# A planner's lengths split into occupation and latency, and VectorE's share of an attention set by a table

## The chip, the cores and the metric

The kernel runs on one core of a Trainium2 chip. The metric is device microseconds of one execution; the median of three runs of the kernel before is 1753.39 us (1752.82 to 1754.59).

## The reference

Four blocks are applied to a residual stream `x` of 2048 tokens by 512 features in bf16: attention, gated mixer, attention, gated mixer, with the same weights both times. Cut to what matters:

```python
def attention(x):            # 32 query heads of 16, one shared key and value head
    q, k, v = heads(x @ wq), x @ wk, x @ wv
    p = softmax(q @ k.T * 16 ** -0.5)          # 32 heads x 2048 x 2048
    return merge(p @ v) @ wo

def mixer(x):                # F = 1792, Fh = 896
    z = gelu(x @ w_in)
    z1, z2 = z[:, :896], layernorm(z[:, 896:])
    g = w_sp @ z2 + b_sp[:, None]              # w_sp is 2048 x 2048
    return (z1 * g) @ w_out

for _ in range(2):
    x = x + attention(layernorm(x))
    x = x + mixer(layernorm(x))
```

The bulk is the exponential of 2 x 32 x 2048 x 2048 scores.

## The kernel before

**Groups and units.** In each layer the attention's queries are cut into 32 groups (`GROUPS`), and each group is worked off in 16 units, one for every 128 keys. A unit is four blocks of 128 keys x 512 query columns, and TensorE computes the four blocks' scores side by side in four row strips of its array (L800). Groups 0 to 3 of a layer (`attn_first`, L975) are interleaved with the projection of keys and values; their partial sums go to an accumulator in SBUF. Groups 4 to 31 follow in `attn_rest` (L991). A group's products with V are summed in one PSUM bank (`PVB`), so that groups follow each other there, and VectorE copies the finished sum out (L923, L926, L932 or L935), after which a short chain normalises and turns it (L902, L908, L917, L945, L948).

**Two ways to take the exponential.** A unit on ScalarE goes through `push_unit` and `push_slot`: blocks are put alternately into a slot of three PSUM banks and one of two, ScalarE takes `Exp` of 1536 or 1024 columns into `P_ring` (L824, a ring of 20 blocks), and TensorE multiplies by V (L841), one step of four matmuls to a unit. A unit on VectorE goes through `push_unit_dve` (L859): the scores go through one of the two side banks, VectorE adds a bias and clamps to an integer of 16 bits (L872, four instructions), makes four further versions with other offsets (L881, four instructions of 128x2048), and TensorE multiplies all five by differently weighted copies of V (L887), five steps of four matmuls. The bits of the integers are read as bf16, and the five together approximate the exponential. The five tiles come from a ring of six (five for the last groups) in `big`.

Which units of a group go to VectorE is given by `UNITS` (the places of 0 to 4 units among the 16) and `ON_DVE` (how many in each group): none in groups 0 to 3, three in 4 to 23, two in 24 to 31. `FIRST_DVE` adds one unit to each of the groups 0 to 3. That is 80 units in a layer and 160 in all.

**Other work under the attention.** The mixer's first products run under the attention as soon as their tokens are done (`b_front`, L1028; evacuated at L1051 and L1077). The product with `w_sp` runs in two stages (`mix_stage`, L1137): stage 0 may start after group 11, stage 1 after group 23. Each stage makes 28 tiles of six steps of four matmuls on TensorE (L613), which VectorE adds up (L1176) and a DMA on SP's queue writes to a scratch tensor (L1178). They have the lowest priority. What remains, and `gelu_rest` and `mix_late`, forms the handover between the layers and the tail after the last one.

**Who orders the work.** The kernel is not written in the order in which it runs. Each operation is recorded with an engine, a length `dur`, a latency `lat`, a priority and the keys that it reads and writes. `schedule` (L174) then plays the whole program through with these lengths before anything is built: an engine that is free takes the ready operation of the best priority (`pick`, L256), a PSUM task takes its banks when they are free in that playing (`banks_for`), and an operation counts as finished for others at its start plus `dur` plus `lat` plus `SEM_LAT` (0.06). The order so found is emitted as each engine's fixed program, with semaphore waits for the real dependencies. The lengths therefore decide the order alone; on the chip an engine waits at the head of its program for whatever is late. Where TensorE has nothing ready and has worked less than 55% of the last 3.4 us of the playing, `filler` (L287) puts in a matmul without effect (L631, L636, and L639 in four strips).

The lengths that matter here: VectorE's operations have their whole length as `dur` and no latency (`dve`, L590). An `Exp` of n blocks has `0.065 + n * 0.4267` and no latency; a PSUM bank comes free in the playing when the task's last operation counts as finished (L386).

Of the kernel before, what the change touches and what calls it, by code (L numbers as in the profile page):

```python
# [10 lines left out]
ALU = mybir.AluOpType  # L11
# [28 lines left out]
SEM_LAT = 0.06  # L40
BESIDE = 0.03

HOLDS = 2.5


# [30 lines left out]
class _Op:  # L76
    __slots__ = ("eng", "fn", "dur", "lat", "prio", "seq", "deps", "succ", "nleft", "chan", "chan_val",
                 "inc", "pos", "val", "clock", "t0", "task", "mode", "rows", "work", "opens", "nstart", "due", "chain")

    def __init__(self, eng, fn, dur, lat, prio, seq, chan, task, mode):  # L80
        self.task = task
        self.mode = mode
        self.rows = frozenset()
        self.work = dur
        self.opens = None
        self.eng = eng
        self.fn = fn
        self.dur = dur
        self.lat = lat
        self.prio = prio  # L90
        self.seq = seq
        self.deps = {}
        self.succ = []
        self.nleft = 0
        self.chan = chan
        self.chan_val = 0
        self.inc = False
        self.pos = -1
        self.val = 0
        self.clock = None  # L100
        self.t0 = -1.0
        self.chain = False
        self.nstart = 0
        self.due = 0.0


class _Graph:
# [66 lines left out]
    def schedule(self):  # L174
# [154 lines left out]
        while True:  # L329
            moved = True  # L330
            while moved:
                moved = False
                for e in ENGS:
                    if free[e]:
# [24 lines left out]
                        push(now + us, 0, e)  # L359
                        push(now + us + o.lat + SEM_LAT, 1, o)  # L360
                        at = now + us + o.lat + SEM_LAT
                        for s, k in o.succ:
# [10 lines left out]
            while ev and ev[0][0] <= now + 1e-9:  # L373
# [3 lines left out]
                elif what == 1:  # L377
                    for s, k in x.succ:
                        if k == 1:
                            met(s, x)  # L380
                    t = x.task
                    if t is not None:
                        t.left -= 1
                        if t.left == 0:
                            for b in t.banks:
                                bank_free[b] = True  # L386
        assert done == len(self.ops), (done, len(self.ops))
# [74 lines left out]
def bass_interleave_layers__grouped_kv_mqa__mixer_gmlp__prompt_kernel(  # L462
# [127 lines left out]
    def dve(fn, us, r, w, prio=5):  # L590
        return op("dve", fn, us, r=r, w=w, prio=prio)

# [210 lines left out]
    def push_slot(n):  # L803
# [19 lines left out]
        def act_e(e):  # L823
            return e.activation(P_ring[:, s0:s0 + n, :], bank32(b0, n).rearrange("p (k q) -> p k q", k=n), ACTF.Exp,  # L824
                                scale=E_SCALE)
        main["last"] = op("act", act_e, 0.065 + n * 0.4267, r=[tk], w=[("P", s0 + k) for k in range(n)], prio=3)
        for k, (u, j) in enumerate(blocks):
# [31 lines left out]
    def push_unit_dve(u):  # L859
# [6 lines left out]
        for j in range(4):  # L866
# [6 lines left out]
                ph16[:, tiles[0], j * QC:(j + 1) * QC], bank32(tk.bank), PH_BIAS, 0.0, op0=ALU.add, op1=ALU.max),  # L873
                0.66, [tk], BIG(tiles[0]) if j == 0 else [("phj", tiles[0], j)], P_R)
            if j == 0:
# [4 lines left out]
        for a in range(1, NPH):  # L880
            dve(lambda e, a=a: e.tensor_scalar(ph16[:, tiles[a], :], ph16[:, tiles[0], :], float(PH_A[a]), None,  # L881
                                               op0=ALU.add), 0.63, base, BIG(tiles[a]), 4)
        for a in range(NPH):
# [107 lines left out]
    def attn_rest():  # L991
        phr["base"] = 0
        for gi in range(NFIRST, len(GROUPS)):
            on_dve = UNITS[ON_DVE[gi]]
            phr["ring"] = NRING if gi < SHORT_RING else NPH
# [285 lines left out]

    UNITS = {0: (), 1: (4,), 2: (3, 8), 3: (2, 6, 10), 4: (2, 5, 8, 11)}

# [4 lines left out]
    NFIRST = 2 * CHUNKS[0][1]  # L1288
    FIRST_DVE = ({12: (2,)}, {12: (2,)})
    KEYS = ((0, 2), (2, 2), (4, 4), (8, 4), (12, 4))  # L1290
# [11 lines left out]
    SLOTS_LATE = ((0, 1, 2, 3, 4, 5, 6), (7, 12, 13, 14, 15, 4, 5, 6), (0, 1, 2, 3, 4, 5, 6, 7, 12, 13, 14, 15))  # L1302
    ON_DVE = [0] * NFIRST + [3] * 20 + [2] * 8
    now = {}
# [63 lines left out]
```

## Time and profile before

| | |
|---|---|
| median of three runs | 1753.39 us |
| span of the profiled execution | 1750.5 us |
| ACT (ScalarE) busy | 1637.6 us, 1425 instructions |
| PE (TensorE matmul) busy | 1664.3 us, 20010 instructions |
| DVE (VectorE) busy | 1356.0 us, 2457 instructions |
| POOL busy | 90.4 us |
| granted TensorE clock, mean | 0.997 |
| DMA | 104 MB, mean 60 GB/s |

For the profiled execution the span is the only time that is given; what lies around it is put at the 2.9 us by which the median of the runs is longer. Busy time is the union of the instructions' records. On ScalarE and VectorE the record of one instruction reaches into that of the next, so that the mean length of a record is longer than the time from one start to the next. A busy PE is not PE at its peak.

In time, groups 4 to 23 of layer 0 lie at 125 to 605 us, groups 24 to 31 at 605 to 820, the handover at 820 to about 860, groups 4 to 23 of layer 1 at 985 to 1464, groups 24 to 31 at 1464 to 1678, and the tail at 1678 to 1750.

### The profile page before, as it was taken

To read this page: it belongs to the slowest core of one execution; us is meant where nothing else is said; L and a number is where in the kernel's file an instruction comes from. 1 tells how busy PE (TensorE), PEld (TensorE's weight loads), DVE (VectorE), ACT (ScalarE), POOL (GpSimd) and SP (SyncE) were. 2 spreads that over 40 slices of the span, in tenths; PEclk is the share of its full clock that TensorE was granted. 3 is DMA by queue.
4 is the path that set the end of the run, shared out by engine and by line. 5 is a ranking of instruction groups with operands and counts; after the bars stand their busy time and mean duration, and the time that the engine had idled before them with its cause. 6 is when DMAs were issued, how large, how long until landed. Compare 5 with 4: busy or idle time off the path is not lost.

```text
span 1750.5 us, 44624 instructions
## 1 busy us (share of the span) xinstructions
PE 1664.3 (95%) x20010; PEld 579.3 (33%) x20010; DVE 1356.0 (77%) x2457; ACT 1637.6 (94%) x1425; POOL 90.4 (5%) x142
## 2 busy tenths in 40 slices
PE   8899999999999999999999999999999999999989
PEld 4332233332333333333432222333333333333334
DVE  8668788888877778675775987888888887766767
ACT  7999999999999999999659999999999999999970
POOL 2000000000000000000430000000000000000012
PEclk9999999999999999999999999999999999999999
DMA  6841000000100302335410000000000112033263
GB/s 185 225 103 49 1 1 2 1 2 25 41 14 20 106 23 70 124 96 161 144 53 19 2 2 1 2 1 2 7 26 7 53 46 88 15 110 110 98 224 120
DMA packets 94816, 104.22 MB, mean 60 GB/s; under 512 B 39072, under 2 KB 64288, under 8 KB 94624
## 3 DMA queue, kind: packets, MB, share of 16 engines
q1 hardware_dynamic: 94624, 101.37, 18.5%
q8 instruction: 156, 2.56, 0.6%
q14 instruction: 36, 0.29, 0.1%
HBM read 61.51 MB, written 39.85 MB: 58 GB/s over the span
## 4 chain that ended last, share of the span: by engine, by line
ACT 75%; PE 22%; DVE 1%; DMA 1%; issue 0%; SPq 0%; POOL 0%; DVEq 0%
ACT P_ring L824 73%; PE ps_all L613 6%; PE ps_all L800 6%; PE ps_all L618 4%; PE ps_all L841 3%; PE ps_all L887 2%; ACT z2n L1087 1%; PE ps_all L639 1%; ACT z1c L1115 0%; PE ps_all L721 0%; DVE big L1216 0%; DVE xn L714 0%; DMA X<-in_A_x_dram 0%; DVE big L1176 0%; DMA big<-gp_scratch 0%
## 5 line engine op out<-in xcount | busy, mean ns | idle before, releaser
L824 ACT ACTIVATE P_ring<-ps_all 128x1536 bf16<-128x1536 f32 (+1 forms) x1383 | 1571.3, 1325 | 56.5 <-PE ps_all L800 55.2
L800 PE MATMUL ps_all<-qT,kT_rep 32*128 32x512 bf16 x4096 | 637.5, 385 | 69.1 <-ACT P_ring L824 55.8
L872 DVE TENSOR_SCALAR big<-ps_all 128x512 int16<-128x512 f32 x640 | 421.8, 686 | 84.5 <-PE ps_all L800 80.2
L881 DVE TENSOR_SCALAR big<-big 128x2048 int16<-128x2048 int16 x640 | 416.2, 682 | 25.0 <-PE ps_all L887 23.8
L800 PEld LDWEIGHTS ps_all<-qT,kT_rep 32*128 32x128 bf16 x4096 | 159.1, 91 | 586.4 <-ACT P_ring L824 451.7
L841 PE MATMUL ps_all<-P_ring,V_aug 128*32 128x512 bf16 x3456 | 333.4, 389 | 0.8 <-DVE big L926 0.5
L887 PE MATMUL ps_all<-big,V_ph 128*32 128x512 bf16 x3200 | 265.0, 385 | 0.6 <-DVE big L872 0.4
L841 PEld LDWEIGHTS ps_all<-P_ring,V_aug 128*32 128x32 bf16 x3456 | 84.6, 93 | 180.7 <-issue 167.2
L639 PE MATMUL ps_all<-ones,zeros 128*32 128x512 bf16 x1320 | 115.0, 388 | 0.0
L887 PEld LDWEIGHTS ps_all<-big,V_ph 128*32 128x32 bf16 x3200 | 75.8, 95 | 90.5 <-issue 36.1
L613 PE MATMUL ps_all<-xnTA,z2n 128*32 128x512 bf16 x1344 | 92.5, 381 | 0.0
L697 POOL TENSOR_SCALAR ve<-mv 128x1 f32<-128x1 f32 (+3 forms) x40 | 10.6, 266 | 1577.3 <-DVE mv L710 1349.9
L962 DVE TENSOR_TENSOR X<-ps_all,X 128x512 bf16<-128x512 f32 x64 | 44.1, 688 | 40.0 <-PE ps_all L618 26.8
L935 DVE CAST oT<-ps_all 128x512 bf16<-128x512 f32 x56 | 38.7, 690 | 38.2 <-PE ps_all L841 38.0
L1176 DVE TENSOR_TENSOR big<-ps_all,big 128x512 f32<-128x512 f32 x56 | 38.3, 689 | 36.8 <-PE ps_all L613 36.5
L1176 DVE TENSOR_TENSOR big<-ps_all,bsp 128x512 f32<-128x512 f32 x56 | 38.5, 688 | 25.1 <-PE ps_all L613 24.6
L613 PE MATMUL ps_all<-w_in_r,xo 128*32 128x448 bf16 x960 | 57.3, 354 | 0.1
L618 PE MATMUL ps_all<-w_out_r,z1c 128*128 128x512 bf16 x224 | 54.2, 380 | 2.8 <-DVE z1c L1221 2.8
L1051 DVE CAST z2n<-ps_all 128x448 bf16<-128x448 f32 x60 | 37.4, 624 | 24.4 <-PE ps_all L613 22.6
L613 PE MATMUL ps_all<-xo,w_in_r 128*32 128x256 bf16 (+1 forms) x1120 | 52.4, 316 | 0.0
L618 PE MATMUL ps_all<-big,z2n 128*128 128x512 bf16 (+1 forms) x224 | 49.4, 366 | 1.3 <-DVE z2n L1131 1.3
L1077 DVE CAST z1c<-ps_all 128x512 bf16<-128x512 f32 (+2 forms) x56 | 36.6, 657 | 16.4 <-PE ps_all L613 13.6
(97 smaller groups left out, 1130.8 us busy)
## 6 DMA issues: line engine op xcount, KB each, us to landing
gp_scratch<-big SPq DMA_DIRECT2D x112, 256.0 KB, 2.0
big<-gp_scratch SPq DMA_DIRECT2D x105, 256.0 KB, 3.0
z1c<-in_B_w_sp_dram SPq DMA_DIRECT2D x16, 512.0 KB, 5.6
wspt_scratch<-z1c SPq DMA_DIRECT2D x16, 512.0 KB, 5.4
xnTA<-wspt_scratch SPq DMA_DIRECT2D x16, 384.0 KB, 4.1
big<-wspt_scratch SPq DMA_DIRECT2D x8, 512.0 KB, 5.8
z2n<-wspt_scratch SPq DMA_DIRECT2D x4, 768.0 KB, 4.8
z1c<-wspt_scratch SPq DMA_DIRECT2D x4, 768.0 KB, 5.6
```

The costliest lines, as they stand in the source:

```text
L613: ins = e.matmul(out_[32 * j:32 * j + 32, :], lhs[:, 32 * j:32 * j + 32], rhs, tile_position=(0, 32 * j), start=start, stop=stop)
L618: return e.matmul(out_, lhs, rhs, start=start, stop=stop)
L639: ins = e.matmul(bank32(PVB)[32 * j:32 * j + 32, :], zeros[:, 0:32], mv, tile_position=(0, 32 * j), start=False, stop=False)
L800: return e.matmul(out, kT_rep[32 * j:32 * j + 32, a, u[1] * P:(u[1] + 1) * P], qT[32 * j:32 * j + 32, q, :], tile_position=(32 * j, 0), st ...
L824: return e.activation(P_ring[:, s0:s0 + n, :], bank32(b0, n).rearrange("p (k q) -> p k q", k=n), ACTF.Exp, scale=E_SCALE)
L841: ins = e.matmul(bank32(PVB)[32 * j:32 * j + 32, :], V_aug[:, kt, :], P_ring[:, s, :], tile_position=(0, 32 * j), start=first, stop=last)
L872: o = dve(lambda e, j=j, tk=tk: e.tensor_scalar(ph16[:, tiles[0], j * QC:(j + 1) * QC], bank32(tk.bank), PH_BIAS, 0.0, op0=ALU.add, op1=AL ...
L881: dve(lambda e, a=a: e.tensor_scalar(ph16[:, tiles[a], :], ph16[:, tiles[0], :], float(PH_A[a]), None, op0=ALU.add), 0.63, base, BIG(tiles ...
L887: ins = e.matmul(bank32(PVB)[32 * j:32 * j + 32, :], V_ph[:, a, kt, :], big[:, tiles[a], j * QC:(j + 1) * QC], tile_position=(0, 32 * j), ...
L935: dve(lambda e: e.tensor_copy(oT[:, par, :], bank32(PVB)), 0.69, ["pvb"], [("oT", par)], 0)
L962: dve(lambda e: e.tensor_tensor(X[:, t, :], bank32(tk.bank), X[:, t, :], ALU.add), 0.69, [tk, ("X", t)], [("X", t)], prio)
L1176: dve(lambda e, part=part, tk=tk: e.tensor_tensor(part, bank32(tk.bank), part if st else bsp[:], ALU.add), 0.69, [tk] + ([] if st else ["b ...
```

## The change

It has two parts. The first gives the playing other lengths: an operation on VectorE is 0.085 shorter in `dur` and has 0.085 as `lat`; an `Exp` has `0.051 + n * 0.4267` as `dur` and 0.185 as `lat`, and its PSUM banks come free in the playing without the latency (`free_lat`). L872's and L881's full lengths go from 0.66 and 0.63 to 0.69. The second replaces `ON_DVE` by a table with a row for each layer, and adds an entry for five units to `UNITS`. The sum is 82 units in a layer beside the four of `FIRST_DVE`: 172 in all. No instruction takes another form.

By groups 4-7, 8-11, ... 28-31 the units were 12, 12, 12, 12, 12, 8, 8 in each layer. They become 16, 15, 13, 13, 13, 5, 7 in layer 0 and 15, 14, 15, 9, 14, 6, 9 in layer 1.

```diff
+DVE_LAT = 0.085
+ACT_LAT = 0.185
+UNITS = {0: (), 1: (4,), 2: (3, 8), 3: (2, 6, 10), 4: (2, 5, 8, 11), 5: (2, 4, 7, 9, 12)}
+ON_DVE = ((0, 0, 0, 0, 4, 4, 3, 5, 3, 4, 4, 4, 4, 3, 4, 2, 4, 2, 4, 3, 4, 3, 3, 3, 2, 1, 0, 2, 1, 3, 2, 1),
+          (0, 0, 0, 0, 4, 4, 3, 4, 3, 4, 4, 3, 4, 4, 3, 4, 2, 2, 1, 4, 3, 4, 3, 4, 1, 2, 1, 2, 2, 2, 2, 3))
...
                         push(now + us + o.lat + SEM_LAT, 1, o)
+                        if o.task is not None:
+                            push(now + us + (o.lat if o.free_lat is None else o.free_lat) + SEM_LAT, 3, o.task)
...
-                    t = x.task
-                    if t is not None:
-                        t.left -= 1
-                        if t.left == 0:
-                            for b in t.banks:
-                                bank_free[b] = True
+                elif what == 3:
+                    x.left -= 1
+                    if x.left == 0:
+                        for b in x.banks:
+                            bank_free[b] = True
...
     def dve(fn, us, r, w, prio=5):
-        return op("dve", fn, us, r=r, w=w, prio=prio)
+        return op("dve", fn, max(us - DVE_LAT, 0.06), r=r, w=w, prio=prio, lat=DVE_LAT)
...
-        main["last"] = op("act", act_e, 0.065 + n * 0.4267, r=[tk], w=[("P", s0 + k) for k in range(n)], prio=3)
+        main["last"] = op("act", act_e, 0.051 + n * 0.4267, r=[tk], w=[("P", s0 + k) for k in range(n)], prio=3,
+                          lat=ACT_LAT)
+        main["last"].free_lat = 0.0
...
-                0.66, [tk], BIG(tiles[0]) if j == 0 else [("phj", tiles[0], j)], P_R)
+                0.69, [tk], BIG(tiles[0]) if j == 0 else [("phj", tiles[0], j)], P_R)
...
-                                               op0=ALU.add), 0.63, base, BIG(tiles[a]), 4)
+                                               op0=ALU.add), 0.69, base, BIG(tiles[a]), 4)
...
-            on_dve = UNITS[ON_DVE[gi]]
+            on_dve = UNITS[ON_DVE[now["layer"]][gi]]
...
-    ON_DVE = [0] * NFIRST + [3] * 20 + [2] * 8
```

## The prediction

> **What bounds the kernel now.** I read the page first, then the chain of waits stretch by stretch, then the groups and the order in time. On the page (section 1, and the chain by engine and by line):
>
> ```profile
> PE 1664.3 (95%) x20010; PEld 579.3 (33%) x20010; DVE 1356.0 (77%) x2457; ACT 1637.6 (94%) x1425; POOL 90.4 (5%) x142
> ACT 75%; PE 22%; DVE 1%; DMA 1%; issue 0%; SPq 0%; POOL 0%; DVEq 0%
> ```
>
> Three engines look full. The chain says which one matters: ScalarE for three quarters, TensorE for most of the rest. Where each holds it, the chain of four stretches shows (125 to 605, 716 to 820, 985 to 1464 and 1464 to 1576 us):
>
> ```profile
> by line: ACT P_ring L824 92.7%; PE ps_all L800 2.2%; PE ps_all L887 1.2%; ACT z2n L1087 1.0%; PE ps_all L841 0.9%; PE ps_all L613 0.8%; PE ps_all L639 0.3%; ACT L1087 0.3%; ACT L824 0.3%; DVE big L1176 0.1%; issue 0.1%; PE ps_all L902 0.1%;
> ...
> by line: PE ps_all L613 30.8%; ACT P_ring L824 27.4%; PE ps_all L800 20.4%; PE ps_all L841 11.8%; PE ps_all L887 5.3%; PE ps_all L618 1.6%; PE ps_all L721 0.8%; DVE big L1176 0.7%; PE ps_all L902 0.6%; PE ps_all L945 0.4%; PE ps_all L639 0.
> ...
> by line: ACT P_ring L824 80.9%; PE ps_all L800 6.7%; PE ps_all L613 4.0%; PE ps_all L841 2.5%; PE ps_all L887 2.3%; PE ps_all L639 1.5%; ACT z2n L1087 1.0%; ACT L1087 0.3%; ACT L824 0.3%; PE ps_all L945 0.2%; issue 0.2%; DVE oT L935 0.1%; P
> ...
> by line: ACT P_ring L824 73.8%; PE ps_all L613 17.0%; PE ps_all L800 6.0%; PE ps_all L841 1.8%; PE ps_all L887 1.3%; PE ps_all L945 0.4%; PE ps_all L636 0.4%; PE ps_all L639 0.3%; issue 0.2%
> ```
>
> In groups 4 to 23 the `Exp` of L824 is the kernel's pace. In groups 28 to 31 of layer 0 it has only 27%, TensorE some 70%; in the other two late stretches (605 to 716 and 1576 to 1678) the same query gives ScalarE 76% and 63%. VectorE is on the chain nowhere, so a unit moved to it pays where ScalarE has the chain. The lengths, from the chain, the order in time (VectorE, TensorE) and the page's groups:
>
> ```profile
> 165.86 162.07 ACT P_ring L824 x143
> ...
> 132.41 2.49 DVE L881 TENSOR_SCALAR big<-big 128x2048 int16<-128x2048 int16 x4
> ...
> 1682.45 3.21 PE L613 MATMUL ps_all<-xnTA,z2n 128*32 128x512 bf16 x56
> ...
> L872 DVE TENSOR_SCALAR big<-ps_all 128x512 int16<-128x512 f32 x640 | 421.8, 686 | 84.5 <-PE ps_all L800 80.2
> L881 DVE TENSOR_SCALAR big<-big 128x2048 int16<-128x2048 int16 x640 | 416.2, 682 | 25.0 <-PE ps_all L887 23.8
> ```
>
> 143 exponentials in 162.07 us are 1.133 us each; they hold 2.5 blocks on average, so a block is 0.453 us and a unit of four 1.81 us. Four L881 take 2.49 us though one record has 0.682: the starts are (2.49 - 0.682) / 3 = 0.603 apart, and VectorE is taken for 8 x 0.603 = 4.83 us by a unit, not for the 5.47 that the records add up to. 14 TensorE steps of four take 3.21, less one record of 0.38 that is 0.217 a step.
>
> **The change part by part.** Counted in the order that the changed kernel is laid in: exponentials 1383 to 1364 (blocks 3456 to 3408), L872 and L881 640 to 688 each, L887's steps 800 to 860, L841's 864 to 852, fillers in strips (L639) 330 to 225, other fillers 94 to 69.
>
> *ScalarE in groups 4 to 23.* Ten units fewer in layer 0, seven in layer 1: -18.1 and -12.7 us. Weighted by ScalarE's share of the chain there (0.927 and 0.809): -16.8 and -10.3. The share is where I choose: ends are the full amounts and nothing. The moved units' extra steps for V (four each, 0.217) are 8.7 and 6.1 us of TensorE; at its share (some 0.055 and 0.17) +0.5 and +1.0.
>
> *VectorE in the same groups.* It gets 82 us more there. What else it does in a block of four groups I count in the new order (instructions times the page's mean record less the 0.08 overlap); low-priority work is laid later than before (stage 0's 28 tiles of L1176 almost all behind group 19 in layer 0, 17 of them within groups 4 to 23 before, six now). Units times 4.83 plus other work, against the block's present stretch less 1.81 for each unit that ScalarE loses:
>
> - Layer 0, groups 4-7: 16.0 x 4.83 + 9.7 = 87.0 against 95.0 - 7.2 = 87.8.
> - Groups 8-11: 15.4 x 4.83 + 12.9 = 87.3 against 90.6. Groups 12-15: 81.6 against 99.2.
> - Layer 1, groups 4-7: 15.0 x 4.83 + 10.8 = 83.3 against 87.6; 8-11: 83.8 against 90.4; 12-15: 83.1 against 97.6.
>
> VectorE fits, in the first block by 1% only. I charge +1 us; ends 0 and the +24 of the second rival.
>
> *Late groups (24 to 31).* ScalarE takes units back: in layer 0 three in groups 24-27 and one in 28-31, in layer 1 two and minus one. At 1.81 and the stretch's share: 5.4 x 0.76 + 1.8 x 0.27 + 3.6 x 0.74 - 1.8 x 0.63 = +6.1. The tiles of `mix_stage` that were put off land here: L1176 goes 16 to 25, 18 to 21, 15 to 22 and 17 to 16 in the four blocks. Six steps of 0.217 a tile, less four steps for a unit taken away: TensorE +9.1, +3.0, +7.4, -0.4 us. At TensorE's shares (0.19, 0.71, 0.27, 0.37): +1.7 +2.1 +2.0 -0.1 = +5.7. Cover is time in which TensorE waits at its head for a bank of L824, 29 us in 605 to 716, and fillers that drop out; without that cover it would be +19 us alone (third rival).
>
> *Fillers.* They sit where TensorE is idle in the playing, yet L639 has 0.3% and 1.5% of the chain in the two long stretches, 8.6 us. 105 of 330 go: -2.7; ends 0 and -8.6.
>
> *Handover and tail.* Of stage 1's steps, 136 matmuls lay behind the last score of layer 0 and 112 behind that of layer 1; now 120 and 80, 12 steps or 2.6 us less in front of the DMA that `mix_late` waits for. I take -1.5; ends 0 and -2.6.
>
> *The rest of the new lengths* adds and removes no instruction and costs nothing by itself: the playing's 0.605 for VectorE and 1.331 and 0.904 for the exponentials stand nearer to the starts in the trace than the old lengths. The earlier freeing of banks puts TensorE at the head of its queue for the next scores sooner than ScalarE's record ends; behind that wait stand L841, L887 and L613. It is what TensorE does already, 452 us in 1110 waits, and those waits hold up others only in the late groups. POOL has 5% of the span, and SP issues the same DMAs, the scratch writes later.
>
> Sum: -27.1 +1.5 +1 +6.1 +5.7 -2.7 -1.5 = -17.0. Against the profiled execution that is a span of 1733.5 for 1750.5; with the 2.9 us by which the median of the runs exceeds it, **1736 us**, 1.0% less.
>
> **The rivals.**
>
> *The order gets better than its units.* An `Exp` of three blocks and one of two, started without a gap, take 1.331 + 0.904 = 2.235 us from start to start; the chain has 2.267. The new lengths could win half of the 0.032 in 682 pairs, 11 us: 1725. For: the old lengths were wrong by just these latencies. Against: 2.267 holds over stretches in which ScalarE waits for nothing visible.
>
> *VectorE becomes the bound (slower).* In 125 to 220 us the waits have
>
> ```profile
> DVE oT L935 <- PE ps_all L841: 6.2, 2, 5.9
> DVE big L872 <- PE ps_all L800: 5.0, 10, 1.7
> ```
>
> Five us of waiting for scores in 55 / 4 units are 0.36 a unit. If these waits stay though VectorE is late, because its two side banks or TensorE's order cause them, the need rises by 0.36 a unit and by the block's waits for L841 (6.2, 3.8, 4.2 and 2.9): 99.0 against 87.8, 96.6 against 90.6, 92.9 against 87.6, 91.8 against 90.4, together +24 in place of +1: 1759, 0.3% slower. It decides once VectorE is late by more than some 18 us in all. For: the 1% of room, a group of five units (24 us for a stretch of 20), a ring of tiles that holds little more than one unit. Against: group 4 of layer 0 already carries 3.8 units in 23.4 us, and the chain there is ScalarE alone.
>
> *TensorE alone sets the late groups.* Then they lengthen by its 19 us and not by 11.8: 1743. For: the 70% in 716 to 820. Against: ScalarE's 74 and 76% in the blocks that take most of the tiles.
>
> *VectorE's records do not overlap when it is full.* A unit is then 5.47 us, the other work an eighth more: 98.5, 98.8, 94.3 and 94.9 against the same stretches, +30: 1765. The four L881 in 2.49 us speak against it. The Trainium skill ("VectorE: DVE Perf Modes", Terms, DRAIN) has a rule that the next operation can't issue until the pipe of the one before is empty; by that rule the records would stand end to end. The trace agrees only so far as that a start follows the last by 0.603 us, and not with a whole record of 0.682.
>
> That the change doesn't do what it says is ruled out by the counts of the new order.
>
> **How the numbers follow.** Chances: the forecast 0.54, a better order 0.12, TensorE late 0.15, VectorE bound 0.15, no overlap 0.04. The first three are faster, 0.81; I take 0.04 off for their upper edges, and a third of the VectorE case lies near no change. So faster by over 0.2% 0.77, within 0.2% (3.5 us, about what a measurement of this kernel can tell) 0.08, slower 0.15. The range runs from 1723, the better order with a part of the fillers' far end, to 1756, which leaves out most of the two VectorE cases.
>
> **What would show it.** Right: the chain of 125 to 605 and 985 to 1464 stays with L824, these stretches shorten by some 16 and 10 us, and the two late ones lengthen by 5 to 10 in layer 0. Wrong: VectorE's lines or TensorE's waits for L872 on the chain at groups 4 to 11, ScalarE's waits there of more than a few us, or late stretches in which L613 holds the chain and the gain is given back.

## The result, and the profile after

The changed kernel takes 1734.52 us (median of four runs, 1731.16 to 1737.31); the kernel before took 1753.99 in the four runs beside it (1752.82 to 1755.08). The ratio is 0.988 (95% interval 0.986 to 0.991). The forecast was 1736. The profiled execution is the shortest of the four, 1731.16 us with a span of 1729.3, where the sum had put 1733.5.

The page of the changed kernel, with busy time and count of each engine and then the shares of the chain by engine:

```profile
PE 1648.7 (95%) x19757; PEld 576.7 (33%) x19757; DVE 1398.0 (81%) x2553; ACT 1617.0 (94%) x1406; POOL 93.6 (5%) x142
ACT 77%; PE 18%; DVE 3%; DMA 1%; issue 0%; POOL 0%; SPq 0%; DVEq 0%
```

ScalarE holds the chain as before, VectorE has 3% of it for 1%. Line numbers after are 9 to 11 higher: `Exp` is L833, scores L809, V for ScalarE's units L852 and for VectorE's L898, VectorE's two steps L883 and L892, the `w_sp` tiles L622 and L1187. The chain in the stretches that the prediction showed, 128 to 590, 710 to 816, 978 to 1444 and 1444 to 1560 us:

```profile
by line: ACT P_ring L833 89.5%; PE ps_all L809 2.8%; PE ps_all L898 1.3%; PE ps_all L622 1.1%; PE ps_all L852 1.1%; ACT z2n L1098 1.0%; PE ps_all L648 0.7%; DVE big L883 0.6%; DVE big L892 0.6%; ACT L1098 0.3%; ACT L833 0.3%; DVE z1c L1088 
...
by line: ACT P_ring L833 71.7%; PE ps_all L622 14.8%; PE ps_all L809 7.6%; PE ps_all L852 3.9%; ACT z2n L1118 2.3%; ACT L1118 1.2%; PE ps_all L730 0.8%; issue 0.2%; PE ps_all L956 0.2%; PE ps_all L648 0.2%
...
by line: ACT P_ring L833 91.1%; PE ps_all L809 1.9%; DVE big L883 1.1%; ACT z2n L1098 1.0%; PE ps_all L898 1.0%; PE ps_all L852 0.9%; DVE big L892 0.9%; PE ps_all L622 0.8%; PE ps_all L648 0.3%; ACT L1098 0.3%; ACT L833 0.3%; PE ps_all L913
...
by line: ACT P_ring L833 63.0%; PE ps_all L622 19.8%; PE ps_all L809 9.0%; PE ps_all L852 4.6%; PE ps_all L898 2.0%; PE ps_all L730 1.0%; PE ps_all L956 0.4%; PE ps_all L627 0.3%; PE ps_all L648 0.3%; PE ps_all L913 0.3%; issue 0.1%
```

In groups 4 to 23 `Exp` still has nine tenths. In 710 to 816 the shares have changed places: TensorE's 70% of before are now 27%. Yet only one unit has come back there (VectorE has 7 for 8), and ScalarE is as busy as before, by the windows of these groups before and after (us of the stretch; busy us and count of PE, PEld, DVE, ACT and POOL; granted clock; DMA share; GB/s):

```profile
716.00:820.00 104.00, 102.24 (x1419) 37.51 (x1415) 67.04 (x118) 101.91 (x90) 1.75 (x4) 1.00 0.37 119
...
710.00:816.00 106.00, 104.01 (x1456) 37.78 (x1457) 64.15 (x112) 104.00 (x93) 2.10 (x4) 1.00 0.44 136
```

It is 98% in both. So the share of the chain can move far with hardly a change of load: of two engines that are both nearly full, the chain names the one that ended last. The pace of `Exp` and the groups answer the lengths:

```profile
178.62 284.22 ACT P_ring L833 x251
...
L883 DVE TENSOR_SCALAR big<-ps_all 128x512 int16<-128x512 f32 x688 | 450.5, 683 | 58.0 <-PE ps_all L809 53.5
L892 DVE TENSOR_SCALAR big<-big 128x2048 int16<-128x2048 int16 x688 | 445.7, 680 | 11.8 <-PE ps_all L898 10.0
```

251 exponentials in 284.22 us are 1.132 each (1.133 before): the order did not make `Exp` faster, there are fewer of them. Of VectorE's waits, the columns are the line, what it waited for, total us, times and the longest; in 128 to 223 us:

```profile
DVE big L883 <- PE ps_all L809: 1.5, 4, 0.7
DVE oT L946 <- PE ps_all L852: 0.7, 1, 0.7
```

Before, the same two waits took 5.0 and 6.2 us. The second rival needed them to stay.

The stretches of the two profiled executions, in us. "First" is groups 0 to 3, with the handover in layer 1:

| stretch | before | after | difference | the prediction's terms |
|---|---|---|---|---|
| layer 0, first | 124.7 | 128.4 | +3.7 | none |
| layer 0, groups 4-23 | 480.0 | 461.9 | -18.1 | -16.8 + 0.5 + 1 |
| layer 0, groups 24-31 | 215.3 | 225.3 | +10.0 | +4.6 and +3.8, ScalarE's and TensorE's parts |
| handover and layer 1, first | 165.5 | 162.2 | -3.3 | -1.5 with the tail |
| layer 1, groups 4-23 | 478.5 | 466.1 | -12.4 | -10.3 + 1.0 |
| layer 1, groups 24-31 | 214.5 | 218.0 | +3.5 | +1.5 and +1.9 |
| tail | 72.0 | 67.4 | -4.6 | see above |
| sum | 1750.5 | 1729.3 | -21.2 | -17.0, with -2.7 for fillers |

Windows of groups 4 to 23, layer 0 and layer 1, of the kernel before and then of the changed kernel (columns as above):

```profile
124.70:604.70 480.00, 457.74 (x5641) 147.42 (x5641) 398.39 (x716) 478.26 (x420) 6.43 (x10) 1.00 0.06 20
985.50:1464.00 478.50, 458.01 (x5695) 149.09 (x5694) 396.75 (x711) 475.73 (x417) 5.72 (x10) 1.00 0.05 16
...
128.40:590.30 461.90, 440.97 (x5410) 142.07 (x5410) 430.90 (x783) 459.54 (x403) 7.73 (x10) 1.00 0.02 5
977.80:1443.90 466.10, 447.16 (x5501) 145.15 (x5502) 418.28 (x761) 463.74 (x407) 5.84 (x10) 0.99 0.05 15
```

ScalarE's busy time falls by 18.7 and 12.0 us, and the stretches by as much.

### The profile page after: what moved, and what is told of

It reads as the page before. It is cut to its first block, busy times and chain, and to the rows that moved or that the text cites. A ratio compares the mean times of both kernels' runs of the same rounds, so it can differ in the third digit from the quotient of the medians.

```text
span 1729.3 us, 44208 instructions
## 1 busy us (share of the span) xinstructions
PE 1648.7 (95%) x19757; PEld 576.7 (33%) x19757; DVE 1398.0 (81%) x2553; ACT 1617.0 (94%) x1406; POOL 93.6 (5%) x142
## 4 chain that ended last, share of the span: by engine, by line
ACT 77%; PE 18%; DVE 3%; DMA 1%; issue 0%; POOL 0%; SPq 0%; DVEq 0%
ACT P_ring L833 75%; PE ps_all L622 5%; PE ps_all L809 4%; PE ps_all L627 4%; PE ps_all L852 2%; PE ps_all L898 1%; ACT z2n L1098 1%; DVE big L883 0%; ACT z1c L1126 0%; DMA wspt_scratch<-z1c 0%; DVE big L892 0%; DVE xn L723 0%; PE ps_all L648 0%; DVE big L1227 0%; DVE st L718 0%
## 5 line engine op out<-in xcount | busy, mean ns | idle before, releaser
L833 ACT ACTIVATE P_ring<-ps_all 128x1536 bf16<-128x1536 f32 (+1 forms) x1364 | 1550.3, 1332 | 58.5 <-PE ps_all L809 57.7
L809 PE MATMUL ps_all<-qT,kT_rep 32*128 32x512 bf16 x4096 | 636.4, 385 | 59.8 <-ACT P_ring L833 44.7
L883 DVE TENSOR_SCALAR big<-ps_all 128x512 int16<-128x512 f32 x688 | 450.5, 683 | 58.0 <-PE ps_all L809 53.5
L892 DVE TENSOR_SCALAR big<-big 128x2048 int16<-128x2048 int16 x688 | 445.7, 680 | 11.8 <-PE ps_all L898 10.0
L809 PEld LDWEIGHTS ps_all<-qT,kT_rep 32*128 32x128 bf16 x4096 | 160.0, 91 | 568.2 <-ACT P_ring L833 449.7
L852 PE MATMUL ps_all<-P_ring,V_aug 128*32 128x512 bf16 x3408 | 331.8, 388 | 2.0 <-DVE oT L943 0.7
L898 PE MATMUL ps_all<-big,V_ph 128*32 128x512 bf16 x3440 | 292.0, 384 | 0.3 <-DVE big L883 0.2
L852 PEld LDWEIGHTS ps_all<-P_ring,V_aug 128*32 128x32 bf16 x3408 | 85.3, 93 | 167.9 <-issue 148.4
L898 PEld LDWEIGHTS ps_all<-big,V_ph 128*32 128x32 bf16 x3440 | 81.2, 95 | 110.3 <-issue 43.2
L622 PE MATMUL ps_all<-xnTA,z2n 128*32 128x512 bf16 x1344 | 90.5, 381 | 0.0
L1187 DVE TENSOR_TENSOR big<-ps_all,bsp 128x512 f32<-128x512 f32 x56 | 38.5, 687 | 53.1 <-PE ps_all L622 53.0
L648 PE MATMUL ps_all<-ones,zeros 128*32 128x512 bf16 x900 | 80.9, 392 | 0.0
L1187 DVE TENSOR_TENSOR big<-ps_all,big 128x512 f32<-128x512 f32 x56 | 38.5, 687 | 46.4 <-PE ps_all L622 46.1
L622 PE MATMUL ps_all<-w_in_r,xo 128*32 128x448 bf16 x960 | 56.7, 353 | 0.8 <-DVE xo L734 0.8
L622 PE MATMUL ps_all<-xo,w_in_r 128*32 128x256 bf16 (+1 forms) x1120 | 53.2, 316 | 0.4 <-DVE big L883 0.2
L1062 DVE CAST z2n<-ps_all 128x448 bf16<-128x448 f32 x60 | 37.3, 621 | 13.1 <-PE ps_all L622 10.9
L1232 POOL TENSOR_TENSOR z1c<-big,z1c 128x512 bf16<-128x512 f32 (+1 forms) x40 | 44.9, 1132 | 52.9 <-DVE big L1227 42.2
```

Source lines behind the costliest of these rows:

```text
L622: ins = e.matmul(out_[32 * j:32 * j + 32, :], lhs[:, 32 * j:32 * j + 32], rhs, tile_position=(0, 32 * j), start=start, stop=stop)
L648: ins = e.matmul(bank32(PVB)[32 * j:32 * j + 32, :], zeros[:, 0:32], mv, tile_position=(0, 32 * j), start=False, stop=False)
L809: return e.matmul(out, kT_rep[32 * j:32 * j + 32, a, u[1] * P:(u[1] + 1) * P], qT[32 * j:32 * j + 32, q, :], tile_position=(32 * j, 0), st ...
L852: ins = e.matmul(bank32(PVB)[32 * j:32 * j + 32, :], V_aug[:, kt, :], P_ring[:, s, :], tile_position=(0, 32 * j), start=first, stop=last)
L883: o = dve(lambda e, j=j, tk=tk: e.tensor_scalar(ph16[:, tiles[0], j * QC:(j + 1) * QC], bank32(tk.bank), PH_BIAS, 0.0, op0=ALU.add, op1=AL ...
L898: ins = e.matmul(bank32(PVB)[32 * j:32 * j + 32, :], V_ph[:, a, kt, :], big[:, tiles[a], j * QC:(j + 1) * QC], tile_position=(0, 32 * j), ...
```

## The experiments

The theory was the prediction's: ScalarE's units moved away in groups 4 to 23 are the gain, VectorE just fits, and the late groups give a part of it back. The rivals: the lengths alone bring it; or any spread of 172 units brings it. When the first runs came out otherwise, the question became why this table with these lengths gains and its halves lose.

Each ratio is to the kernel before on the same chip. One and the same version scatters here by some us, and the granted clock of TensorE falls to half for windows of 3.41 us, a varying number of them. Within the 13 versions, 82 runs, the time goes with the mean clock at -1.25 us per 0.001 (correlation -0.96). The last column uses this price to move the difference of the medians to the mean clock of before in the same chip's runs (0.995 to 0.996; for the changed kernel, beside whose runs no clocks of before are on record, 0.9957). It is an estimate, and differences of 2 or 3 us in it mean nothing. "Behind" is the number of steps (four matmuls) of stage 1 that the order lays behind the last scores of layer 0 and of layer 1; by this count the kernel before has 42 and 28. In layer 0 the traces have 6 to 10 fewer behind the last score, 34 for the kernel before and 30 for the changed kernel, which are the prediction's 136 and 120 matmuls; in layer 1 the two counts agree. Where one number stands for a version it is the sum of both layers.

| version | median us | ratio, 95% | mean clock | behind | at before's clock |
|---|---|---|---|---|---|
| changed kernel | 1734.52 | 0.988 (0.986-0.991) | 0.993 | 36, 20 | -23 |
| e1 lengths, old units | 1767.98 | 1.008 (1.006-1.011) | 0.989 | 62, 12 | +6 |
| e2 table, old lengths | 1770.12 | 1.010 (1.008-1.012) | 0.992 | 10, 0 | +12 |
| e3 172 units evenly | 1770.56 | 1.010 (1.008-1.012) | 0.991 | 104, 98 | +12 |
| e4 four in each group | 1774.79 | 1.013 (1.011-1.015) | 0.992 | | +17 |
| e5 changed, more fillers | 1747.48 | 0.996 (0.994-0.997) | 0.991 | 56 | -12 |
| e6 e1, more fillers | 1760.11 | 1.003 (1.002-1.004) | 0.994 | 74 | +5 |
| e7 even, 12 late | 1753.70 | 1.000 (0.998-1.002) | 0.988 | 60, 60 | -9 |
| e8 table, 16 late | 1764.70 | 1.006 (1.005-1.008) | 0.988 | 110, 62 | +2 |
| e9 e3, half of stage 1 | 1743.66 | 0.995 (0.993-0.997) | 0.991 | 31, 19 | -17 |
| e10 VectorE's lengths | 1743.89 | 0.993 (0.992-0.995) | 0.990 | 36, 12 | -18 |
| e11 ScalarE's lengths | 1780.37 | 1.015 (1.014-1.017) | 0.991 | 36, 78 | +20 |
| e12 later landing | 1739.66 | 0.992 (0.989-0.994) | 0.990 | 36, 20 | -22 |

### The two halves of the change

e1 keeps the new lengths and puts the old units in the table:

```diff
-ON_DVE = ((0, 0, 0, 0, 4, 4, 3, 5, ...), (0, 0, 0, 0, 4, 4, 3, 4, ...))
+ON_DVE = ((0, 0, 0, 0, 3 in each of 20 groups, 2 in each of 8),) * 2
```

> The changed kernel's lengths with the old numbers of units (3 in groups 4 to 23, 2 in 24 to 31: 160 in all). Theory (the gain is ScalarE's time for 12 units, 21.8 us, and the lengths by themselves give nothing): within 3 us of the kernel before, 1751 to 1757, exponentials of 691 + 691 + 1 as before. Rival (the order is what got better): at least half of the gain without a unit moved, 1744 or less.

It is 15 us slower than before, outside both forecasts. Groups 4 to 23 are as they were (482.0 and 478.2 us); the start grows by 6.2 and the handover with the first groups by 5.5. Windows of e1 from 0 to 130.9 and from 829.4 to 1000.4 us (columns as above):

```profile
0.00:130.90 130.90, 118.23 (x1266) 49.36 (x1266) 89.04 (x182) 112.70 (x99) 11.73 (x36) 0.93 0.70 188
829.40:1000.40 171.00, 158.89 (x1435) 60.09 (x1427) 122.26 (x229) 130.07 (x114) 38.32 (x48) 0.99 0.25 78
```

The clock at the start is 0.93 (0.99 before), and in this whole trace it is at half for 41 us, in the one of before for 10.2. By the estimate of the table 9 of the 15 us go with the clock, and some 6 us of loss are left.

e2 is the kernel before with the new table. Against the changed kernel it has the old lengths (the main lines; L892's goes back too):

```diff
-        return op("dve", fn, max(us - DVE_LAT, 0.06), r=r, w=w, prio=prio, lat=DVE_LAT)
+        return op("dve", fn, us, r=r, w=w, prio=prio)
...
-        main["last"] = op("act", act_e, 0.051 + n * 0.4267, ..., lat=ACT_LAT)
-        main["last"].free_lat = 0.0
+        main["last"] = op("act", act_e, 0.065 + n * 0.4267, ...)
...
-                0.69, [tk], BIG(tiles[0]) ...
+                0.66, [tk], BIG(tiles[0]) ...
```

> The new table of 172 units laid with the old lengths. Theory (units alone): the whole gain, 1732 to 1738. Rival (the table needs the lengths, because the old ones count a unit on VectorE longer than it is and put its steps in the wrong places): 1742 or more, with VectorE's or TensorE's waits in groups 4 to 11.

The same units, moved to the same groups, now lose 17 us, as the rival had it. Windows of e2, groups 4 to 23 of both layers, then its waits of ScalarE in 125 to 410 us:

```profile
124.80:608.70 483.90, 455.65 (x5670) 147.68 (x5670) 439.46 (x790) 462.00 (x404) 7.96 (x10) 1.00 0.05 14
995.80:1482.80 487.00, 462.87 (x5827) 149.60 (x5827) 427.64 (x769) 465.25 (x408) 7.00 (x10) 1.00 0.06 19
```

```profile
ACT P_ring L824 <- PE ps_all L800: 21.6, 17, 5.9
```

ScalarE's work has gone down to 462.0 us as in the changed kernel (459.5), but the stretch has not: it waits for scores, 21.6 us where the kernel before had 1.6 and the changed kernel 2.1 (128 to 410 us). In layer 0 that is 22 us against the changed kernel (483.9 less 461.9), in layer 1 it is 21. This is what the prediction's second rival looks like from ScalarE. The chain shows VectorE on the path, in 125 to 410 us of e2 and then in 128 to 410 of the changed kernel:

```profile
by line: ACT P_ring L824 69.6%; PE ps_all L800 6.4%; PE ps_all L887 3.8%; PE ps_all L613 3.7%; DVE big L872 3.5%; DVE big L881 3.4%; PE ps_all L841 2.6%; ACT z2n L1087 1.6%; PE ps_all L639 0.8%; DVE z1c L1077 0.7%; DVE st L709 0.6%; issue 0
...
by line: ACT P_ring L833 93.8%; PE ps_all L809 1.5%; DVE big L883 1.1%; DVE big L892 1.1%; PE ps_all L898 0.7%; PE ps_all L648 0.6%; PE ps_all L852 0.5%; PE ps_all L622 0.3%; DVE X L973 0.2%; DVE qT L783 0.2%; DVE st L718 0.2%; PE ps_all L9
```

VectorE itself waits too:

```profile
DVE big L872 <- PE ps_all L800: 12.1, 29, 1.8
```

It is busy for 439 of 484 us and waits 12.1 for scores in 125 to 410. The kernel before waits 10.8 us there for the same, but VectorE had a lighter load. So VectorE is late for TensorE at times and TensorE is late for VectorE at others, though VectorE is not full. The new table needs the lengths, which the prediction priced at nothing.

Which lengths? e10 keeps VectorE's new ones and has ScalarE's old one; e11 the reverse:

```diff
 e10
-        main["last"] = op("act", act_e, 0.051 + n * 0.4267, ..., lat=ACT_LAT)
-        main["last"].free_lat = 0.0
+        main["last"] = op("act", act_e, 0.065 + n * 0.4267, ...)
 e11
-        return op("dve", fn, max(us - DVE_LAT, 0.06), r=r, w=w, prio=prio, lat=DVE_LAT)
+        return op("dve", fn, us, r=r, w=w, prio=prio)
...
-                0.69, [tk], ...       (L885, and L893 from 0.69 to 0.63)
+                0.66, [tk], ...
```

> The new table with VectorE's new lengths and ScalarE's old ones (0.065, no latency, banks freed as before). Steps behind the attentions: 36 and 12. Theory (the table needs VectorE's lengths, and ScalarE's give nothing): 1730 to 1738. Rival (ScalarE's latency is what puts TensorE's products at the right place): 1745 or more, with more waits of TensorE for L833.

> The new table with ScalarE's new lengths and VectorE's old ones (0.66 and 0.63, no latency apart). Steps behind the attentions: 36 and 78. Theory (the playing then holds VectorE for longer than it is and lays TensorE's steps late): 58 steps more in the tail and ScalarE waiting in groups 4 to 15 as with all the old lengths, 1755 to 1770. Rival (VectorE's lengths do not matter): 1740 or less.

The same view, ScalarE's waits in 130 to 410 us, of e10 and then of e11:

```profile
ACT P_ring L833 <- PE ps_all L809: 9.7, 10, 1.7
```

```profile
ACT P_ring L833 <- PE ps_all L809: 26.4, 12, 6.7
```

Without VectorE's new lengths the waits of e2 are there again, and e11 is 26 us slower than before. Its trace is 49 us longer than the changed kernel's: 26 in groups 4 to 23 of layer 0 (487.9 us), 5 in those of layer 1, and 17 in the tail (84.3 us), behind which 78 steps are laid for 20. With VectorE's lengths and ScalarE's old ones (e10) the waits are less than half and the kernel 10 us faster than before, at before's clock 18 of the changed kernel's 23; it falls between the two forecasts. VectorE's length is the part that counts; ScalarE's adds some 5 us by the estimate. The playing counted a unit at 4 x 0.66 + 4 x 0.63 = 5.16 us of VectorE and counts it at 8 x 0.605 = 4.84 now; the chip takes 4.83. With the old figure VectorE would be early for its scores on the chip, and TensorE's fixed order would serve both engines at the wrong times. The waits of both in e2 fit that; that the figure works in this way is argued, not shown. No run tells the shorter hold of the engine from the latency behind it, as both went together. It may also be that the table suits the one order it was laid with. Against that, three versions with this table and VectorE's new lengths, but another order, keep 12 to 22 of the 23 us at before's clock (e5, e10, e12), and the two with VectorE's old lengths lose 35 and 43 (e2, e11).

### The table: how many units, and where

e3 spreads the same 172 units evenly, 66 over groups 4 to 23 and two in each late group; e4 puts four in each of groups 4 to 23 (200 units):

```diff
 e3
+ON_DVE = ((0, 0, 0, 0, 3, 4, 3, 3, 4, 3, 3, 3, 4, 3, 3, 4, 3, 3, 4, 3, 3, 3, 4, 3, 2, 2, 2, 2, 2, 2, 2, 2),) * 2
 e4
+ON_DVE = ((0, 0, 0, 0, 4 in each of 20 groups, 2 in each of 8),) * 2
```

> The new lengths and 172 units, but spread evenly: 3 or 4 in groups 4 to 23 (66), 2 in each of 24 to 31. Theory (the number counts, not the places): ScalarE has the same 3408 blocks, so 1731 to 1738. Rival (the table's catch-up places and its relief of the late groups count): the late groups stay as long as before, but VectorE's put-off work has no place to catch up, 1741 or more.

> The new lengths and four units in every group from 4 to 23, two in 24 to 31: 200 in all. If ScalarE alone set the pace: 28 units x 1.81 = 51 us less than the changed kernel, 1684. Theory (VectorE is full at about 3.6 units a group): 80 units x 4.83 + 77 us of other work = 464 us in groups 4 to 23 of layer 0 where the changed kernel took 462, and 471 against 466 in layer 1, so there no gain, and about 1735 to 1745 in all with VectorE's lines on the chain.

e4 finds the limit. Its groups 4 to 23 of layer 0, and ScalarE's waits there:

```profile
129.90:622.70 492.80, 470.18 (x5924) 156.53 (x5924) 478.36 (x869) 446.76 (x390) 8.88 (x10) 1.00 0.05 15
```

```profile
ACT P_ring L833 <- PE ps_all L809: 44.0, 29, 15.7
```

VectorE is busy for 478.4 of 492.8 us (97%), ScalarE for 446.8. The expectation of about 1735 to 1745 missed: it had counted 464 us for VectorE. 80 units at 4.83 are 386, so the other work is 92 us and not 77, and another 14 us of waiting come on top. The changed kernel is below this limit, with VectorE busy for 93% of the stretch:

```profile
128.40:590.30 461.90, 440.97 (x5410) 142.07 (x5410) 430.90 (x783) 459.54 (x403) 7.73 (x10) 1.00 0.02 5
```

e3 is another loss, as its rival had it. Its groups 4 to 23 are 9.0 and 8.9 us shorter than before and its late groups as before; it loses in the handover (181.2 us with the first groups, against 162.2) and in the tail (88.8 against 67.4). The chain of the handover, 813 to 900 us of e3 and then 815 to 900 us of the changed kernel:

```profile
by line: PE ps_all L627 28.5%; PE ps_all L622 20.9%; PE ps_all L809 9.0%; PE ps_all L852 5.3%; DMA big<-gp_scratch 4.6%; DVE big L1227 3.8%; PE ps_all L1263 3.8%; PE ps_all L1257 3.7%; DMA gp_scratch<-big 3.7%; DVE st L718 3.2%; DVE X L973 
```

```profile
by line: PE ps_all L627 31.7%; ACT P_ring L833 10.0%; PE ps_all L809 9.7%; ACT z1c L1126 9.3%; DVE xn L723 6.2%; PE ps_all L852 5.2%; PE ps_all L1263 3.6%; ACT z2n L1118 2.9%; issue 2.8%; PE ps_all L622 2.4%; DVE X L973 2.2%; DVE big L1227 
```

In e3 the `w_sp` products (L622) hold 20.9% of 87 us, 18 us; in the changed kernel 2.4% of 85, 2 us. Those are the steps of stage 1 for which the attention had no room: 202 of e3's lie behind it, 56 of the changed kernel's. The kernel before also has 16 late units, but 17 and 19 of its `w_sp` tiles ran in groups 4 to 23; in e3, with more units there, 7 and 7. With the 146 steps more, handover and tail are 40.4 us longer, 0.28 a step (e3's clock there is 0.99 and 0.98, the changed kernel's 1.00 in both). In the tail a few steps cost little: with 0, 12, 12 and 20 of them it takes 66.1, 67.6, 66.6 and 67.4 us (e2, e1, e10, changed). The kernel before, with 28, has 72.0. In the changed kernel the Gelu (`z2n` L1118 and `z1c` L1126, 12% of the handover's chain) holds ScalarE meanwhile.

Two versions separate the late units from the rest. e7 is even like e3 but with 12 units in the late groups and 70 before them; e8 is the change's table with two in each late group:

```diff
 e7
+ON_DVE = ((0, 0, 0, 0, 4, 3, 4, 3, ... to group 23, 2, 1, 2, 1, 2, 1, 2, 1),) * 2
 e8
-(..., 2, 1, 0, 2, 1, 3, 2, 1), (..., 1, 2, 1, 2, 2, 2, 2, 3)
+(..., 2, 2, 2, 2, 2, 2, 2, 2), (..., 2, 2, 2, 2, 2, 2, 2, 2)
```

> The new lengths and 172 units, 4 and 3 by turns in groups 4 to 23 and 2 and 1 by turns in 24 to 31. ScalarE has the same blocks as in the changed kernel and in the even spread with 16 late units. Behind the attentions are laid 60 and 60 steps of the second stage, where the even spread had 104 and 98 and the changed kernel 36 and 20. Theory (at equal units the time goes by these steps, 0.217 us each on TensorE's path): 1734.5 + 64 x 0.217 = 1748. Rival (what counts is the table's exact places in groups 4 to 23): 1760 or more, with the loss inside these groups.

> The changed kernel with two units in every group from 24 to 31, 16 in a layer as before the change, in place of 12 and 15: 177 in all. Behind the attentions are laid 110 and 62 steps of the second stage, 116 more than in the changed kernel. Theory (late units are paid in TensorE's steps): 1734.5 + 116 x 0.217 - 5 x 1.81 = 1751. Rival (late units are worth ScalarE's time like any other): 1726.

Both miss their forecasts, e7 between the two and e8 14 us above the higher one. Windows of e8, its late groups of layer 0, the handover with the first groups of layer 1, and the tail:

```profile
592.50:808.50 216.00, 210.46 (x2822) 74.26 (x2823) 149.19 (x268) 211.51 (x183) 5.22 (x10) 1.00 0.26 88
808.50:994.00 185.50, 171.69 (x1628) 67.47 (x1633) 124.78 (x235) 130.51 (x114) 38.56 (x48) 0.97 0.32 99
1680.80:1763.10 82.30, 71.97 (x497) 31.02 (x496) 57.26 (x96) 16.76 (x14) 17.36 (x18) 0.96 0.53 172
```

Four and one more units in the late groups make these 12.6 us shorter together than the changed kernel's (216.0 and 214.7 against 225.3 and 218.0), and handover and tail 38 longer, at clocks of 0.97 and 0.96 for 1.00; groups 4 to 23 of layer 1 are 6.0 longer too. So the units taken from the late groups, which the prediction booked as a cost only, buy room there: the order lays 46 `w_sp` tiles into the late groups of layer 0 in the changed kernel, 34 in e8, 33 in e3. How five units make room for so many steps is not shown; their own extra steps for V are only 20. e7, with 12 late units and no other care for their places, has 43, and its groups 4 to 23 are as short as the change's (462.6 and 457.9). It has 120 steps behind the attentions, where e3 has 202 and the changed kernel 56, and the lowest clock but one, 0.988. At before's clock it would gain 9 us where e3 loses 12 and the table gains 23: moving four units of each layer from the late groups into groups 4 to 23 goes with some 21 of these 35 us. The rest is left for the exact places, which no run tests alone.

e9 tests the same cause the other way: e3 with half of the steps of stage 1 left out.

```diff
+            ns = nb // 2 if st else nb
...
-            products(tk, nb, mk, lambda s: Z2(a0 + s) + rows_of(s)[1], pr, per=2, mode=2)
+            products(tk, ns, mk, lambda s: Z2(a0 + s) + rows_of(s)[1], pr, per=2, mode=2)
```

> The even spread of 172 units (1770.6 us) with half of the second stage's steps left out: three of six in each tile, so the mixer's sums are incomplete. Behind the attentions are laid 31 and 19 steps, where the even spread had 104 and 98 and the changed kernel 36 and 20; groups 4 to 23 have the same work as in the even spread. Theory (the even spread loses by the second stage's steps behind the attentions): handover and tail fall back to the changed kernel's 162 and 67 us from 181 and 89, 1730 +- 6. Rival (it loses by the places of its units): 1750 or more.

27 us of e3's time come back, with 50 steps behind the attentions in place of 202; 1744 is 8 us above the theory's 1730 +- 6 and below the rival's 1750. The profiled execution is its slowest (its handover has a clock of 0.93 and takes 176.2 us) and still has a tail of 72.6 us for 88.8. What it can't show is how much of the 27 us lies under the attention, where steps were left out too.

### The clock, and a wait at the start

e5 and e6 put in fillers where TensorE has worked less than 60% of the last 3.4 us, in place of 55%: e5 in the changed kernel (381 fillers for 294), e6 in e1 (495 for 402).

```diff
-WARM = 0.55
+WARM = 0.60
```

> The changed kernel with fillers wherever TensorE has worked less than 60% of the last 3.4 us of the playing, 55% before: 381 fillers in place of 294, and about as many steps of the mixer's second stage behind the attention (56 in place of 56). Theory (the drops of the granted clock, four in the changed kernel's profile, each cost one to two us): at most two drops and 1728 to 1733. Rival (the drops cost nothing, fillers stand in the way): 1735 or more.

> The new lengths with the old units (1768 us) and the 60% rule for fillers: 495 fillers in place of 402, the same 74 steps of the second stage behind the attentions. Theory (half of what the lengths alone lost are the eight drops of the clock): four drops or fewer and 1756 to 1762. Rival (the loss is in the order itself): 1765 or more.

e6 fell as expected: five half-speed windows in its trace (17 us) for twelve in e1's, and 8 us less. At before's clock e1 and e6 are the same, +6 and +5, so by this estimate the clock is what separates them. e5 went against expectation: ten windows in place of five, and 13 us slower than the changed kernel, 11 of which stay at the same clock; its late groups of layer 1 are 229.6 us for 218.0 (the tail 65.3 for 67.4). More fillers do not reliably hold the clock up. That they take time in a kernel in which TensorE is 95% busy is likely but not shown, as the order changed with them. What sets the windows off is not settled. Windows of the changed kernel about the drop at 1000 to 1007 us:

```profile
980.00:1000.00 20.00, 19.44 (x235) 6.02 (x231) 18.13 (x33) 20.00 (x18) 0.00 (x0) 1.00 0.01 2
1000.00:1020.00 20.00, 19.85 (x191) 5.75 (x183) 17.42 (x34) 17.80 (x17) 0.00 (x0) 0.83 0.01 2
```

The clock fell although TensorE's records fill 19.44 us of the 20 before it and 2.84 of the last 3.4, and ScalarE was then idle for 2.2 us of the next 20.

The 3.7 us at the start of the changed kernel have a wait of their own; from the order in time on VectorE, and the chain of 0 to 128 us:

```profile
75.50 1.29 DVE L1286 COPY z1c<-ps_all 128x1024 bf16<-128x1024 bf16 x2 [5.40 <-DMA wspt_scratch<-z1c]
```

```profile
67.68 7.73 DMA wspt_scratch<-z1c
```

A copy of the transposed `w_sp` stands in front of VectorE's queue for a scratch write that takes longer than the 5.0 us of the playing. e12 gives the playing 6.5:

```diff
-            [("wt", b, 0), ("wt", b, 1)] + Z1ALL, [("wd", tt)], f"wt{b}", 5.0)
+            [("wt", b, 0), ("wt", b, 1)] + Z1ALL, [("wd", tt)], f"wt{b}", 6.5)
```

> The changed kernel with 6.5 in place of 5.0 us for the landing of the transposed w_sp in the playing; the trace has 5.6 in the middle and VectorE waits up to 5.4 us for one at 70 us. Steps behind the attentions as in the changed kernel, 36 and 20. Theory (the 4 us that groups 0 to 3 of layer 0 became longer are this wait): they fall from 128 to 125 us, 1731. Rival (the DMA engines are full there and the order can do nothing): 1734 to 1737.

The start fell by 0.4 us only, to 128.0, and both forecasts missed. At before's clock e12 is no better than the changed kernel (-22 and -23), and its median is 5 us higher. The wait for the DMA is gone there, and the same copies wait 13.4 us for TensorE in 60 to 90 us instead. So the wait is real, but the 3.7 us don't hang on it; the start's clock (0.96 for 0.99, three half-speed windows for one) may account for some 2.5 of them by the price above. No version beat the changed kernel.

## Why the prediction was right, and where its steps were not

**The time and the main term.** 1736 against 1734.5: right, with the place right too. That it is so near is partly luck: by the stretches the terms were off by -3.2 us (groups 4 to 23, with the fillers), +1.7 (late groups), -6.4 (handover and tail) and +3.7 (start), which leaves -4.2. Groups 4 to 23 hold the gain, `Exp` at an unchanged 1.13 us holds their chain, and the late groups give some of it back.

**ScalarE in groups 4 to 23** was mis-sized at -16.8 and -10.3; the stretches fell by 18.1 and 12.4, the full 1.81 us for each of the 10 and 7 units (-18.1 and -12.7). By this the weight was the wrong one: the share of the chain. Where the chain leaves ScalarE for a moment ScalarE still works; by the windows it was busy for 478.3 of 480.0 us and 475.7 of 478.5. The busy share of the stretch, 99%, fits better, and V's extra steps, +0.5 and +1.0, do not show. Two more versions are less exact: e7, with ten units more in each layer, has 17.4 and 20.6 us less (18.1 by the full price), and e3, with six, 9.0 and 8.9 (10.9). So the price is good to some 2.5 us a layer.

**VectorE, +1 us.** Right for this kernel: its waits went down as its load went up, as the count of 4.83 us a unit wanted. The term hung on more than was said. At the old lengths the same units miss by 22 us in layer 0 (e2), and e4 shows the edge at 97% busy.

**The rest of the new lengths "costs nothing by itself"** is the step that failed. They add no instruction, and alone they lose (e1, +6 us at the same clock), but the units lose 12 without them and gain 23 with them. The sum did not suffer, as its counts were read from an order that had been laid with the new lengths; the reason was wrong.

**Late groups.** +11.8 forecast, +13.5 measured (+10.0 and +3.5). The parts were right to 2 us. ScalarE's busy time in layer 0 rose by 8.5 us (211.7 to 220.2; four units are 7.2), and it was 98% busy in the second half before as after. So here too the share of the chain (0.27) was too low a price for a unit, and TensorE's share (0.71) then not all its own. That these groups make room for the `w_sp` tiles, and so decide handover and tail, was seen only from the cost side.

**Handover and tail.** -1.5 forecast, -3.3 and -4.6 measured. 12 to 14 steps fewer at 0.28 would be 3.4 to 3.9 us. But fewer steps still bring little: e2 with 46 fewer than the changed kernel has 162.8 and 66.1 us, the first at a clock of 0.96. How the 7.9 us divide isn't shown.

**Fillers, -2.7,** were not seen as a gain of their own; the two long stretches are explained by the units to 0.3 us. On the chain the strips go from 0.3% and 1.5% (L639) to 0.7% and 0.3% (L648), 8.6 us to 4.6, so some gain in layer 1 is not excluded. e5 is slower with more fillers, with another order in the same step.

**Start,** no term, +3.7: a lower clock goes with it; e12 does not bear out the wait of L1286. It stands against the error in handover and tail, with the other sign, which helped the total.

**The rivals.** The better order (1725) did not come: an exponential takes 1.132 us on average, as before. VectorE as the bound did not come in the changed kernel, and came in e4, at 97% busy. In e2 and e11 ScalarE waits as that rival says, with VectorE busy for 439 of 484 and of 488 us. TensorE alone in the late groups: they lengthened by 13.5 us and not by 19, and ScalarE's busy time there rose by 10.6. Records that do not overlap when VectorE is full: not so either. At 167 to 175 us of the changed kernel VectorE holds the chain, one instruction behind the other, and there stands

```profile
171.21 0.60 DVE big L883
171.81 2.40 DVE big L892 x4
```

five instructions at 0.60 us each, with records of 0.68.

## What to carry to other kernels

Lengths that order a program can be worth as much as the work that is moved: split each into the time that holds the engine (start to start of two in a row) and the rest, and set the split before the shares of the engines are tuned, since the same table lost 1% with the old lengths and gained 1.2% with the new. Price a unit taken from the pacing engine by that engine's busy share of the stretch rather than by its share of the chain, as long as the engine that takes the unit has room. A share that is cut where the engine is full should be judged by where the low-priority work goes that shared it: here 12 and 15 late units in place of 16 made room for 17 tiles (84 in both layers, 67 in e8), whose steps otherwise go with some 0.3 us each in handover and tail.

## What the runs showed of the hardware

The granted clock fell to half for windows of 3.41 us and multiples (up to 20.5 us in the profile of e9), with TensorE busy for 97% of the 20 us and 84% of the last 3.4 us ahead of one. The number went with the version, though not with the number of fillers: the mean clock is 0.996 for before and 0.988 for e7 and e8, and 0.001 of it goes with 1.25 us. The Trainium skill ("TensorE: Matmul & The Clock Gate", Part 1) gives a free-running window of 3413 ns and halving after an idle one. The length agrees with the trace; an idle window ahead of the drop at 1000 us the trace doesn't show, and no run here tells what the gate counted.
